# A last block whose gates change from Sigmoid to exponential and logarithm, and out weights in rotating slots, in a chain of linear attention, a gated layer and soft mixture of experts

## The chip, the cores and the metric

The kernel runs on 1 core of one Trainium2 chip. The metric is the device time of one execution in microseconds. A core has five engines with a queue each: TensorE (PE; PEld is its weight loading), VectorE (DVE), ScalarE (ACT), GpSimd (POOL) and SyncE (SP). Each queue runs its instructions in the order in which they were written; semaphores hold an instruction until what it reads or overwrites is ready. DMA transfers are started from SP's and ACT's queues.

## The reference

Three stages follow each other, all in fp32, on 4 sequences of 576 tokens:

```python
# attention: 4 x 8 heads, 64 wide, 128 features
h = einsum(x * scale, omega) - sum((x * scale)**2) / 2
phi = exp(h - max(h)) / sqrt(128)                 # for q and for k
kv, z = k_phi^T v, sum(k_phi)
x = (q_phi kv) / (q_phi z + 1e-6)                 # 2304 tokens x 512
# gated layer, 512 -> 1536 -> 512
gate = 1 / (1 + exp(-(x @ w_gate)))
x = (gate * (x @ w_val)) @ w_out
# soft mixture of experts: 8 experts, 4 slots each
logits = x @ phi
d, c = softmax of logits over tokens, softmax of logits over slots
slot_in = d.T @ x
slot_out[e] = relu(slot_in[e] @ w1[e]) @ w2[e]
out = c @ slot_out
```

`w_gate`, `w_val` and `w_out` arrive as 8-byte floats and are narrowed in the kernel.

## The kernel before

The 2304 tokens are cut into blocks: four of 512 (blocks 0 to 3, each the first 512 tokens of a sequence) and block 4 of 256, the last 64 tokens of each sequence. The attention works on 16 units of two heads (u = 0 to 15). The gated layer has 12 slices of 128 of its hidden dimension (f = 0 to 11). Nearly all its products are exact to fp32 by splitting each operand into a high part (rounded to fp32r) and a low part (the rest), and taking three products (`three`). A weight piece (`wscr[f]`, part 0 gate, 1 value, 2 out) is loaded into `WR`, six slots of 512 columns shown as `ws`, then split by a cast (`hi_of`, on ACT or DVE) and a subtraction (`lo_of`, on POOL or DVE).

The order is: attention for units 0 to 3, then block 0 for f < 6, block 1, block 0's other f (GROUPS; interleaved with the later units), then blocks 2 and 3 together as a pair (`pair_jobs`), then block 4, the last block (steps i >= LAST), then the experts. In `pair_jobs`, six steps of two f each make gate and value for both blocks with seven products in place of eight (`pair_up`), and block 2's out products. Then a stretch planned at SPAND = 33 us makes block 3's out products alone, for which the out weights of all f are loaded once more in pairs (`pair_load(f, 2, at)` into slots at and at + 1). At its end come the first loads of the last block's pieces (`load_part(k)` into slot k). In the last block each piece that has been split starts the load of the piece six later in its place.

A gate of the blocks before 2 is made from the sum `s` in PSUM by absolute value, exponential, logarithm, one DVE operation and an exponential: exp(min(s, 0) - ln(1 + exp(-abs(s)))). The pair and the last block use ACT's Sigmoid. ACT holds one table of functions at a time; an `ACT_TABLE_LOAD` changes it. Its first table, natural_log_exp_and_others, is loaded by name at the start; all other loads are put in by the compiler where the next function isn't in the table. Exponentials of the experts' softmax (`chunk_logits`, `weights`, `join_slots`, `last_slots`) stand among the Sigmoids.

The order on each queue is not that of the code. Every operation is recorded with its reads, its writes and a due time (`plan.t` less a lead), and a list scheduler (`Plan.schedule`) runs them in a model with a cost for each and gives each engine the ready operation that is due first; ACT's change of table is in it (RELOAD). The whole order is then issued from one line, which is why L425 is the line of every instruction in the profile. Names tell them apart: `ga` and `va` are the banks of gate and value, `o0` to `o3` those of the out products, `fl` others; `ga_a` the gate in SBUF (and, in the pair, split out weights of odd f), `gt` the gated product in two parts, `w0` to `w2` the split weights; `x2T` and `x` (x2) a block's result and its transposed copy, brought back by 16 DMAs of SP (`chunk_back`). The experts' first weights w1 are loaded from ACT's queue, w2 from SP's.

The gate in the last block and the choice of slots before:

```python
        if i >= LAST:
            ACT.activation(out=a, in_=ps, func=AF.Sigmoid)
            return a
...
        places = [4, 2, 0, 4, 2, 4]
```

At the tail (`last_slots`), block 4's logits, their maximum, the exponential of `dt` (ACT), the slots' sums `ps` in bank o0 and then the experts follow each other; a few products without use (`warm`, bank va) are put between.

Of the kernel before, what the change touches and what calls it, by code (L numbers as in the profile page):

```python
# [20 lines left out]
B, H, S, D, M = 4, 8, 576, 64, 128  # L21
# [3 lines left out]
NF = DFF // 128  # L25
# [7 lines left out]
PAIR = (2, 3)  # L33
# [12 lines left out]
W_LO = float(np.uint32(0x38000000).view(np.float32))  # L46
BIG = 3.0e38
W_HI = float(np.uint32(0x47EFFFFF).view(np.float32))

# [31 lines left out]
READY = 12.0  # L81
EARLY = 6.0
LEAD = {
# [28 lines left out]
class Plan:  # L112
# [135 lines left out]
    def schedule(self):  # L248
# [109 lines left out]
        while ev:  # L358
# [13 lines left out]
            for e in E:  # L372
                while free_at[e] <= now + 1e-9:
# [21 lines left out]
                    c, held = self.cost(e, alt[1], alt[3], outs, ins)  # L395
                    want = {AF.Exp: 0, AF.Ln: 0, AF.Sigmoid: 1}.get(alt[3].get("func"), table) if e == "ACT" else table
                    if want != table:
                        c, table = c + RELOAD, want
# [33 lines left out]
def body(ctx, tc, nc, qkT, tok, von, omT, wall, phi, w1, w2, ident_d, srep_d, rrep_d, mask_d, out):  # L432
# [87 lines left out]
    Vs = [carve(g3, 896 * k + 128, [NT, 2, 64]) for k in range(2)]  # L520
    QTF = carve(g3, 2560, [2, S])
    obf = carve(g3, 3712, [256])
    QY = carve(g3, 1792, [512])
    HKs = [carve(r, 0, [4, 2, M]) for r in (g4, q2)]
# [110 lines left out]
    def chunk_qT(u, i):  # L635
        if u >= N_SPLIT and i < 2:
            turn_q(u, i)
            return
        ps = bank().rearrange("p (h n) -> p h n", h=2)
        n, k = ((256, 0), (256, 0), (64, 64))[i]  # L640
        for h in range(2):
            if i == 2:
                PE.transpose(ps[:, h, 0:128], HTs[u % 2][:, 0, h, :], ident)
                continue
            for t in range(2):
                PE.transpose(ps[:, h, 128 * t:128 * t + 128], HQs[u % 2][:, 2 * i + t, h, :], ident)
        if u < N_NUM:
            copy(QTF[:, :, 256 * i:256 * i + n], ps[:, :, k:k + n], SITE["hqt"])
            return
        qh, ql = (QT[:, l, :, 256 * i:256 * i + n] for l in range(2))  # L650
        hi_of(qh, ps[:, :, k:k + n], SITE["hqt"])
        lo_of(ql, ps[:, :, k:k + n], qh, ("DVE",))

    def turn_q(u, h):

        y = QY.rearrange("p (j t a) -> p t j a", j=4, t=4)
        for t in range(4):
            DVE.transpose(y[:, t], HQs[u % 2][:, t, h].rearrange("p (j a) -> p j a", j=4))
        scr = qscr[2 * (u % 2) + h]
        SP.dma_start(out=scr, in_=QY)  # L660
        d = scr.rearrange("(i a) (j f) -> j a i f", i=4, j=4)
        for j in range(4):
            SP.dma_start(out=QTF[32 * j:32 * j + 32, h, 0:512].rearrange("p (i f) -> p i f", i=4), in_=d[j])
        x = QTF[:, h, 0:512].rearrange("p (i t b) -> p t i b", t=4, i=4)
        qh, ql = (QT[:, k, h, 0:512].rearrange("p (t i b) -> p t i b", t=4, i=4) for k in range(2))
        hi_of(qh, x, SITE["hqt"])
        for t in range(4):
            lo_of(ql[:, t], x[:, t], qh[:, t], ("DVE",))
# [58 lines left out]
    def step_chunks(u):  # L727
# [3 lines left out]
        def P(i):  # L731
            return lambda: chunk_proj(v, i)

        def kv():
            chunk_kv(u)
            prep_qk(v, 1)
            load_unit(u + 2)
# [7 lines left out]
        if v < ROWS:  # L745
            c = [kv, P("K0"), qT[0], P("K1"), qT[1], qT[2], P("T"), num[0], P("Q0"), num[1], last]
            own = (0, 2, 4, 5, 7, 9)
        else:
            c = [kv, P("K"), qT[0], qT[1], qT[2], P("T"), num[0], num[1], last]
            own = (0, 2, 3, 4, 6, 7)  # L750
# [96 lines left out]
    def gate(i):  # L847
        n = BLOCKS[STEPS[i][0]][1]
        ps = up_passes(i, 0, "ga")
        a = T([128, 512], "ga_a", F32, 2)[:, 0:n]  # L850
        if i >= LAST:
            ACT.activation(out=a, in_=ps, func=AF.Sigmoid)
            return a
# [168 lines left out]
    def chunk_logits(j):  # L1022
# [13 lines left out]
        DVE.tensor_scalar(out=neg, in0=new, scalar1=-1.0, scalar2=None, op0=ALU.mult)  # L1036
        DVE.tensor_copy(out=lt[0:p, 1, :], in_=ps)
        ACT.activation(out=lt[0:p, 0, :], in_=ps, func=AF.Exp, bias=neg, accum_out=row)
        if j != DONE[0]:
# [83 lines left out]

    def load_w1():

        e = len(W1)
        if e < E:
            W1.append(pieces(EXTAGS[e], 3 if EXTAGS[e] == "XT" else 1))
            for c in range(4):
                ACT.dma_start(out=W1[e][c], in_=w1[e, :, 1024 * c:1024 * c + 1024])  # L1130

    def load_w2():
# [209 lines left out]
    stream("att", T0)  # L1342
    ACT.preload_act_table_set("natural_log_exp_and_others")
    DVE.memset(g4[:, 0:256], 0.0)
# [106 lines left out]
    def pair_jobs(t):  # L1451
# [34 lines left out]
        for n in range(6):  # L1486
            f, t0 = 2 * n, t + dt * n
            add(t0, lambda f=f, t0=t0: pair_up(f, 0, t0, 0.39 * dt))
            add(t0 + 0.01, lambda f=f: (f + 2 < NF and pair_load(f + 2, 0, 0), pair_split(1)))
            add(t0 + 2.11, lambda f=f: split_out(f, 4))  # L1490
            add(t0 + 0.39 * dt, lambda f=f, t0=t0: pair_up(f, 1, t0 + 0.39 * dt, 0.39 * dt))
            if n < 5:
                add(t0 + 0.39 * dt + 0.01, lambda f=f: (pair_load(f + 2, 1, 2), pair_split(0)))
            add(t0 + 0.39 * dt + 0.02, lambda f=f: split_out(f + 1, 4))
            downs(f, t0 + 0.9 * dt, PAIR[0], "a")
            downs(f + 1, t0 + 1.01 * dt, PAIR[0], "a")
            add(t0 + 0.4 * dt, lambda f=f: pair_load((f + 2) % NF, 2, 4))
        t += SPANQ
        places = [4, 2, 0, 4, 2, 4]
        dt = SPAND / NF  # L1500
        for n in range(6):
            f, at, t0 = 2 * n, places[n], t + SPAND * n / 6
            if n in (0, 1):
                add(t + 0.2 + 0.1 * n, lambda f=f, at=places[n + 1]: pair_load(f + 2, 2, at))
            add(t0 + 0.02, lambda f=f, at=at: (split_out(f, at), late_split(f)))
# [3 lines left out]
            downs(f + 1, t0 + 0.06 + 2 * dt, PAIR[1], "b")  # L1509
            nxt = {0: lambda: pair_load(6, 2, 4), 1: lambda: pair_load(8, 2, 2), 3: lambda: pair_load(10, 2, 4),  # L1510
                   2: lambda: (load_part(0), load_part(1)), 4: lambda: (load_part(2), load_part(3)),
                   5: lambda: (load_part(4), load_part(5))}[n]
            add(t0 + 0.035, nxt)
        add(t + SPAND - 6.0, lambda: (split_w(LAST, 0), split_w(LAST, 1)))
# [10 lines left out]
    for g, (j, f0, f1) in enumerate(GROUPS):  # L1525
        span = SPAN[g]
        if j == NB - 1:
            m2_jobs(0, start + 3.0, 60.0)
            jobs += [(start + 4.0, "ex", load_w1), (start + 12.0, "ex", load_w1)]
            start = pair_jobs(start)  # L1530
            jobs += [(start - SPAND + 1.0 + 8 * k, "ex", load_w1) for k in range(4)]
            m2_jobs(PAIR[0], start - SPAND + 1.0, SPAND * 0.9)
            m2_jobs(PAIR[1], start + span / NF, span * 0.7)
            jobs += [(start - 5.0, "ex", load_w1), (start + 2.0, "ex", load_w1), (start + 8.0, "ex", free_more),
                     (start + span * 0.9, "end", free_halves), (start + span * 0.85, "m2", join_slots)]
# [99 lines left out]
```

## Time and profile before

| | us |
|---|---|
| median of 3 runs | 669.59 |
| lowest and highest of them | 668.32, 669.80 |
| the profiled execution | 666.81 |
| its span, from the first to the last instruction | 664.9 |
| TensorE busy in it | 644.0 |
| VectorE, ScalarE, GpSimd busy in it | 479.7, 410.6, 289.2 |

The profile is of one execution. Its times count from the start of the span. Matmuls are pipelined, so that neighbouring entries overlap and a busy TensorE need not be at its peak. "Idle before" is the time that an engine waited ahead of an instruction, and the name behind the arrow is what ended the wait.

### The profile page before, as it was taken

What the parts mean: (1) busy time and instruction counts of PE and PEld (TensorE: products, weight loads), DVE (VectorE), ACT (ScalarE), POOL (GpSimd) and SP (SyncE); (2) the same over time, 40 slices, a digit from 0 to 9 for tenths busy, and PEclk for the clock granted to TensorE, in tenths of its full rate; (3) what the DMA queues carried; (4) which work ended last, traced back from release to release, by engine and by line L of the source; (5) the groups of instructions that cost most, each with busy time, mean ns of one, the idle gap of its engine ahead of it and who ended that gap; (6) DMA issues with size and microseconds to landing.
All of it is one profiled execution on the core that took longest, in us unless ns stands there. A gap on an engine that the chain in (4) does not pass through costs nothing.

```text
span 664.9 us, 12634 instructions
## 1 busy us (share of the span) xinstructions
PE 644.0 (97%) x4268; PEld 513.2 (77%) x4268; DVE 479.7 (72%) x1379; ACT 410.6 (62%) x937; POOL 289.2 (43%) x272
## 2 busy tenths in 40 slices
PE   7899999999999999999999999999999999899995
PEld 5676777768888888888877778878888779899663
DVE  5898989888998765667689987557557757756323
ACT  4899989889998866777675654534442225445012
POOL 0456344455445344455453555555551453542100
PEclk9999999999999999999999999999999999999998
DMA  7987857678976345223315552222228899777988
GB/s 233 324 269 260 274 188 273 204 237 272 298 260 215 101 115 176 90 97 98 109 49 185 195 147 78 63 64 63 65 65 293 278 316 346 229 233 264 353 334 240
DMA packets 55216, 132.17 MB, mean 199 GB/s; under 512 B 6256, under 2 KB 14192, under 8 KB 55152
## 3 DMA queue, kind: packets, MB, share of 16 engines
q1 hardware_dynamic: 49328, 114.01, 52.7%
q10 hardware_dynamic: 5824, 17.37, 7.7%
q8 instruction: 33, 0.54, 0.3%
q14 instruction: 31, 0.25, 0.1%
HBM read 113.00 MB, written 14.16 MB: 191 GB/s over the span
## 4 chain that ended last, share of the span: by engine, by line
PE 84%; DMA 5%; DVE 4%; ACT 2%; POOL 1%; SPq 1%; issue 1%; DVEq 0%; POOLq 0%; ACTq 0%
PE o L425 24%; PE fl L425 23%; PE va L425 19%; PE ga L425 18%; DMA g<-in_tok 2%; DMA x2T<-x 1%; DMA g<-in_w 1%; DVE g L425 1%; DMA ws<-wscr 1%; SPq L425 1%; DVE XT L425 1%; POOL g L425 1%; DVE ga_a L425 1%; ACT w L425 0%; DMA g<-in_qkT 0%
## 5 line engine op out<-in xcount | busy, mean ns | idle before, releaser
L425 POOL TENSOR_TENSOR w<-ws,w 128x512 fp32r<-128x512 f32 (+1 forms) x101 | 120.6, 1195 | 161.3 <-ACT w L425 67.2
L425 PE MATMUL o<-gt,w 128*128 128x512 f32 (+1 forms) x576 | 134.7, 372 | 2.2 <-POOL w L425 0.9
L425 PEld LDWEIGHTS o<-gt,w 128*128 128x128 f32 x576 | 97.2, 189 | 24.4 <-issue 2.4
L425 PE MATMUL ga<-XT,w 128*128 128x512 f32 (+1 forms) x432 | 101.6, 367 | 0.9 <-POOL XT L425 0.9
L425 ACT ACTIVATE w<-ws 128x512 fp32r<-128x512 f32 (+1 forms) x100 | 57.7, 579 | 72.3 <-PE o L425 28.1
L425 PE MATMUL va<-XT,w 128*128 128x512 f32 (+1 forms) x432 | 100.1, 366 | 1.6 <-DVE ga_a L425 1.1
L425 PE MATMUL fl<-g,g 64*128 64x128 f32 (+4 forms) x686 | 84.1, 313 | 3.5 <-ACT g L425 1.7
L425 ACT ACTIVATE g<-g 128x128 f32<-128x128 f32 (+4 forms) x206 | 73.8, 414 | 16.9 <-DVE g L425 12.9
L425 PEld LDWEIGHTS ga<-XT,w 128*128 128x128 f32 x432 | 69.9, 189 | 16.8 <-issue 4.7
L425 PEld LDWEIGHTS va<-XT,w 128*128 128x128 f32 x432 | 70.5, 189 | 15.2 <-issue 2.4
L425 PEld LDWEIGHTS fl<-g,g 64*128 64x128 f32 (+2 forms) x686 | 60.3, 182 | 24.4 <-issue 7.3
L425 ACT ACTIVATE x2T<-g 128x512 f32<-128x512 f32 x72 | 45.8, 666 | 4.2 <-DVE x L425 2.4
L425 ACT ACTIVATE g1b<-g1b,g 128x128 f32<-128x128 f32 x128 | 40.8, 389 | 5.9 <-DVE g L425 5.7
L425 DVE TENSOR_SCALAR x2T<-x2T 128x512 f32<-128x512 f32 (+1 forms) x72 | 35.9, 513 | 3.7 <-ACT x2T L425 3.4
L425 POOL TENSOR_TENSOR g<-g 128x640 f32<-128x640 f32 (+1 forms) x19 | 23.4, 1230 | 33.3 <-DMA g<-in_tok 13.3
L425 DVE CUSTOM_DVE_ANT_0 g<-fl,g 128x128 f32<-128x128 f32 x142 | 32.3, 286 | 6.5 <-PE fl L425 6.4
L425 PE MATMUL o<-gt,ga_a 128*128 128x512 f32 x144 | 35.4, 393 | 0.0
L425 DVE TENSOR_TENSOR XT<-fl,XT 128x512 f32<-128x512 f32 x24 | 16.6, 690 | 23.0 <-PE fl L425 23.0
L425 POOL TENSOR_TENSOR x<-x2T 128x512 int32<-128x512 int32 x19 | 24.6, 1295 | 16.1 <-DVE x2T L425 11.3
L425 PEld LDWEIGHTS o<-gt,ga_a 128*128 128x128 f32 x144 | 26.7, 188 | 5.8 <-POOL ga_a L425 0.3
L425 ACT ACTIVATE ga_a<-ga_a 128x512 f32<-128x512 f32 x48 | 30.0, 624 | 1.7 <-DVE ga_a L425 1.4
L425 POOL TENSOR_TENSOR w<-x,w 128x512 fp32r<-128x512 f32 x15 | 19.3, 1285 | 24.2 <-DVE x2T L425 11.5
(254 smaller groups left out, 1264.3 us busy)
## 6 DMA issues: line engine op xcount, KB each, us to landing
ws<-wscr SPq DMA_DIRECT2D x42, 512.0 KB, 3.7
g<-in_wall SPq DMA_DIRECT2D x36, 512.0 KB, 5.0
ws<-wscr SPq DMA_DIRECT2D x54, 256.0 KB, 3.7
wscr<-x SPq DMA_DIRECT2D x36, 256.0 KB, 4.6
g<-in_qkT SPq DMA_DIRECT2D x15, 576.0 KB, 5.3
g<-in_tok SPq DMA_DIRECT2D x15, 576.0 KB, 5.1
g<-in_w ACTq DMA_DIRECT2D x16, 512.0 KB, 6.9
XT<-in_w ACTq DMA_DIRECT2D x12, 512.0 KB, 4.6
```

The source lines that it names most:

```text
L425: ins = getattr(self.eng[e], method)(*a, **k)
```

## The change

The Sigmoids of the last block become the chain of the earlier blocks: `i >= LAST` becomes `LAST <= i < SIGS` with SIGS = 0. The table for exponential and logarithm is loaded by name once, ahead of block 2's logits' exponential, recorded as reading their sum and `SG[1]`, which the pair's last Sigmoid writes. Block 3's out weights and the first pieces of the last block go round the three pairs of slots in turn. In the attention, the third chunk of q transposes (the tail's) comes first from unit 3 on; code for a turn through DRAM is cut in two, for units from 16 on. Some numbers get names, with the values that they had.

```diff
+EXP_LN = "natural_log_exp_and_others"
...
-EARLY = 6.0
+SIGS = 0
+W1AT = (1.0, 9.0, 17.0, 25.0, 28.0, 35.0)
+W1FLOOR = (0, 0, 0, 0, 0, 0)
+EARLY = 6
+M2A = -32.0
+M2B = 0.66
+M2C = 3.75
+M2D = 0.7
...
                     want = {AF.Exp: 0, AF.Ln: 0, AF.Sigmoid: 1}.get(alt[3].get("func"), table) if e == "ACT" else table
+                    want = 0 if alt[1].startswith("preload") else want
...
-    QTF = carve(g3, 2560, [2, S])
-    obf = carve(g3, 3712, [256])
-    QY = carve(g3, 1792, [512])
+    QTF = carve(g3, 2688, [2, S])
+    obf = carve(g3, 3840, [256])
+    QYs = carve(g3, 1792, [2, 512])
+    QLs = carve(g3, 2816, [2, 512])
...
         if u >= N_SPLIT and i < 2:
-            turn_q(u, i)
+            split_q(i)
             return
...
         def kv():
+            if u >= N_SPLIT:
+                turn_q(u, 0)
+                turn_q(u, 1)
             chunk_kv(u)
...
-            c = [kv, P("K"), qT[0], qT[1], qT[2], P("T"), num[0], num[1], last]
+            c = [kv, P("K"), qT[2], qT[0], qT[1], P("T"), num[0], num[1], last]
...
-        if i >= LAST:
+        if LAST <= i < SIGS:
             ACT.activation(out=a, in_=ps, func=AF.Sigmoid)
             return a
         ACT.activation(out=a, in_=ps, func=AF.Abs)
...
         DVE.tensor_copy(out=lt[0:p, 1, :], in_=ps)
+        if j == PAIR[0] and SIGS < NS:
+            plan.place([("ACT", "preload_act_table_set", (EXP_LN,), {})], [lt[0:p, 0, :]], [ps, SG[1]])
         ACT.activation(out=lt[0:p, 0, :], in_=ps, func=AF.Exp, bias=neg, accum_out=row)
...
-            add(t0 + 0.01, lambda f=f: (f + 2 < NF and pair_load(f + 2, 0, 0), pair_split(1)))
+            add(t0 + 0.01, lambda f=f: (pair_load(f + 2, 0, 0) if f + 2 < NF else pair_load(2, 2, 0), pair_split(1)))
...
-            if n < 5:
-                add(t0 + 0.39 * dt + 0.01, lambda f=f: (pair_load(f + 2, 1, 2), pair_split(0)))
+            add(t0 + 0.39 * dt + 0.01, lambda f=f: (pair_load(f + 2, 1, 2), pair_split(0)) if f + 2 < NF else pair_load(4, 2, 2))
...
-        places = [4, 2, 0, 4, 2, 4]
+        places = [4, 0, 2, 4, 0, 2]
...
-            if n in (0, 1):
-                add(t + 0.2 + 0.1 * n, lambda f=f, at=places[n + 1]: pair_load(f + 2, 2, at))
...
-            nxt = {0: lambda: pair_load(6, 2, 4), 1: lambda: pair_load(8, 2, 2), 3: lambda: pair_load(10, 2, 4),
-                   2: lambda: (load_part(0), load_part(1)), 4: lambda: (load_part(2), load_part(3)),
-                   5: lambda: (load_part(4), load_part(5))}[n]
-            add(t0 + 0.035, nxt)
+            if n < 3:
+                add(t0 + 0.035, lambda f=f, at=at: pair_load(f + 6, 2, at))
+            else:
+                add(t0 + 0.035, lambda at=at: (load_part(at), load_part(at + 1)))
```

## Rows read from the trace of the kernel before

**Rows 1.** The page's head, TensorE: busy us (share of the span), instructions.

```profile
PE 644.0 (97%) x4268; PEld 513.2 (77%) x4268; DVE 479.7 (72%) x1379; ACT 410.6 (62%) x937; POOL 289.2 (43%) x272
```

**Rows 2.** Stretches: length, busy PE, PEld, DVE, ACT, POOL, clock, DMA share, GB/s.

```profile
60.00:70.00 10.00, 8.41 (x56) 6.93 (x57) 9.29 (x38) 9.41 (x25) 7.11 (x8) 1.00 0.85 284
560.00:580.00 20.00, 17.70 (x141) 16.92 (x141) 14.62 (x35) 10.69 (x18) 9.49 (x8) 1.00 0.80 224
585.70:607.30 21.60, 21.60 (x181) 20.63 (x180) 13.58 (x30) 10.02 (x17) 9.94 (x8) 1.00 0.66 216
```

**Rows 3.** Who TensorE waited for in 500 to 620: us, times, longest.

```profile
PE va L425 <- DVE ga_a L425: 1.1, 1, 1.1
PE o L425 <- POOL w L425: 0.9, 2, 0.7
PE va L425 <- POOL w L425: 0.5, 1, 0.5
```

**Rows 4.** TensorE's instructions in time: start us, us, operation, count, idle before.

```profile
538.41 2.56 PE L425 MATMUL o<-gt,w 128*128 128x512 f32 x10 [0.46 <-DVE w L425]
...
585.68 1.60 PE L425 MATMUL ga<-XT,w 128*128 128x256 f32 x12
...
591.45 1.60 PE L425 MATMUL va<-XT,w 128*128 128x256 f32 x12
...
614.13 1.06 PE L425 MATMUL va<-dt 128*128 128x128 f32 x8
615.34 1.97 PE L425 MATMUL o<-dt,x 128*128 128x32 f32 x16
```

**Rows 5.** ScalarE's groups after 512, up to 340, whole, in 560 to 572.

```profile
L425 ACT ACT_TABLE_LOAD x9 | 11.5, 1283 | 1.5 <-PE o L425 1.3
...
L425 ACT ACT_TABLE_LOAD x1 | 1.3, 1283 | 0.7 <-PEq L1630 0.7
L425 ACT ACTIVATE ga_a<-ga_a 128x512 f32<-128x512 f32 x44 | 27.5, 624 | 1.6 <-DVE ga_a L425 1.2
L425 ACT ACTIVATE ga_a<-ga_a,one_b 128x512 f32<-128x512 f32 x22 | 15.7, 716 | 0.2
...
L425 ACT ACTIVATE ga_a<-ga 128x256 f32<-128x256 f32 x12 | 4.6, 382 | 5.5 <-PE ga L425 4.7 <-DVE w L425 0.8
...
L425 ACT ACT_TABLE_LOAD x4 | 5.1, 1283 | 0.2
```

**Rows 6.** ScalarE's instructions in time.

```profile
330.15 0.62 ACT L425 ACTIVATE w<-ws 128x512 fp32r<-128x512 f32 x1
...
535.80 1.15 ACT L425 ACTIVATE w<-ws 128x512 fp32r<-128x512 f32 x2 [1.56 <-DMA ws<-wscr]
...
577.40 0.63 ACT L425 ACTIVATE w<-ws 128x512 fp32r<-128x512 f32 x1 [5.91 <-DMA ws<-wscr]
...
607.90 0.38 ACT L425 ACTIVATE ga_a<-ga 128x256 f32<-128x256 f32 x1
...
613.74 1.28 ACT L425 ACT_TABLE_LOAD   x1
615.03 0.26 ACT L425 ACTIVATE dt<-dt 128x64 f32<-128x64 f32 x1
```

**Rows 7.** VectorE: a group's count, busy time and mean; then instructions in time.

```profile
L425 DVE CAST gt<-ga_a 128x256 fp32r<-128x256 f32 x11 | 6.0, 547 | 0.2
...
575.98 0.43 DVE L425 CAST w<-ws 128x512 fp32r<-128x512 f32 x1 [2.26 <-DMA ws<-wscr]
...
588.84 0.42 DVE L425 TENSOR_TENSOR ga_a<-va,ga_a 128x256 f32<-128x256 f32 x1 [0.87 <-PE va L425]
589.29 0.29 DVE L425 CAST gt<-ga_a 128x256 fp32r<-128x256 f32 x1
...
614.24 0.22 DVE L425 TENSOR_TENSOR dt<-o,cs 128x64 f32<-128x64 f32 x1
```

**Rows 8.** Who SyncE's queue waited for in 559 to 564: us, times, longest.

```profile
SPq L425 <- DMA g<-in_w: 3.2, 2, 2.5
```

More of the change, by code (lines that the diff above doesn't have):

```diff
@@ L654, in turn_q @@
     def turn_q(u, h):
-        y = QY.rearrange("p (j t a) -> p t j a", j=4, t=4)
+        y = QYs[:, h].rearrange("p (j t a) -> p t j a", j=4, t=4)
         for t in range(4):
@@ L659, in turn_q, with split_q @@
         scr = qscr[2 * (u % 2) + h]
-        SP.dma_start(out=scr, in_=QY)
+        SP.dma_start(out=scr, in_=QYs[:, h])
         d = scr.rearrange("(i a) (j f) -> j a i f", i=4, j=4)
         for j in range(4):
-            SP.dma_start(out=QTF[32 * j:32 * j + 32, h, 0:512].rearrange("p (i f) -> p i f", i=4), in_=d[j])
-        x = QTF[:, h, 0:512].rearrange("p (i t b) -> p t i b", t=4, i=4)
+            SP.dma_start(out=QLs[32 * j:32 * j + 32, h].rearrange("p (i f) -> p i f", i=4), in_=d[j])
+    def split_q(h):
+        x = QLs[:, h].rearrange("p (i t b) -> p t i b", t=4, i=4)
         qh, ql = (QT[:, k, h, 0:512].rearrange("p (t i b) -> p t i b", t=4, i=4) for k in range(2))
@@ L1122, in pieces, with load_w1 @@
         return [t[:, 1024 * c:1024 * c + 1024] for c in range(n)]
-    def load_w1():
+    def load_w1(k=None):
         e = len(W1)
+        plan.floor = 0.0 if k is None else W1FLOOR[k]
         if e < E:
@@ L1130, in load_w1 @@
                 ACT.dma_start(out=W1[e][c], in_=w1[e, :, 1024 * c:1024 * c + 1024])
+        plan.floor = 0.0
     def load_w2():
@@ L1342, in body @@
     stream("att", T0)
-    ACT.preload_act_table_set("natural_log_exp_and_others")
+    ACT.preload_act_table_set(EXP_LN)
     DVE.memset(g4[:, 0:256], 0.0)
@@ L1530, in body @@
             start = pair_jobs(start)
[L1531 to L1534, printed above, removed]
+            jobs += [(start - SPAND + x, "ex", lambda k=k: load_w1(k)) for k, x in enumerate(W1AT)]
+            m2_jobs(PAIR[0], start + M2A, span * M2B)
+            m2_jobs(PAIR[1], start + M2C, span * M2D)
+            jobs += [(start + 8.0, "ex", free_more),
                      (start + span * 0.9, "end", free_halves), (start + span * 0.85, "m2", join_slots)]
```

## The prediction

> **What bounds the kernel now.** I read the page's head first: TensorE is busy 97% of the span [rows 1]. So only time in which TensorE waits can come back; the change takes no matmul away. Then the table by stages says where it waits: 1.6 of 10 us at the start around 60 to 70, 2.3 of 20 in 560 to 580, and nothing in 585.7 to 607.3 [rows 2]. The waits of TensorE in 500 to 620 name the releasers: 1.1 us for VectorE's product `ga_a`, 0.9 and 0.5 for GpSimd's low parts of weights [rows 3]. These 2.5 us are the waits of 560 to 585; TensorE's own list adds one of 0.46 for VectorE's low part at 538.41 [rows 4]. Together 3.0 us: about all that the out-weight slots and the gates can win on TensorE ahead of the tail.
>
> The profiled execution took 666.81 us, 1.91 more than its span; the median of the runs shown is 669.59, 2.78 above it. I make the sum as a difference on the profiled execution and set it on the median.
>
> **Table loads.** After 512 us the trace has 9 loads of ScalarE's function tables at 1283 ns; in the first 340 us it has 1, though 22 gates ran there with exponential, logarithm and exponential again [rows 5]: the table loaded there by name holds both. So one load by name should serve the whole end, and 8 of the 9 go: 8 x 1.28 = 10.3 us of ScalarE. ScalarE has slack there, so the sum looks at where a load holds something up.
>
> At the tail, the load of 613.74 ends where the exponential of `dt` starts, 615.03 [rows 6]. Its input was ready at 614.24 + 0.22 = 614.46 [rows 7]. TensorE starts the slot products at 615.34, behind 8 warming matmuls that end at 614.13 + 1.06 = 615.19 [rows 4]. Without the load the products could start near 614.8. If the order keeps the warming ahead, 615.34 - 615.19 = 0.15 is won; if not, 615.34 - 614.8 = 0.5. I take -0.3, between them. A switch cost 615.03 - 613.74 = 1.29 us there [rows 6]. The Trainium skill (ScalarE: Activation LUTs, What ACT_TABLE_LOAD costs) counts some 2.66 us for each switch to another set, a drain included. The trace shows no such drain behind this load; by that figure the tail's term would be larger by 1.4 us at most, and the sum -2.9.
>
> At the last gate, two loads with one small exponential between, 2.6 us, put its Sigmoid at 607.90 [rows 6]. The chain below is 1.9 us longer than a Sigmoid and so takes less than the loads' place: 0, with no gain either, since the out products and the joining of the slots cover it.
>
> The load by name stands in ScalarE's queue ahead of the exponential of block 2's logits, behind the last Sigmoid. It takes the place of the first of the 9, and block 3's out products cover it on TensorE: 0. Behind it in the queue wait casts of out weights; were that cover gone, it would cost 1.28.
>
> **The gates of the last block.** Each of 12 Sigmoids (382 ns [rows 5]) becomes an absolute value, an exponential, a logarithm, a VectorE operation and an exponential. Durations by rows: the absolute value as the Sigmoid, which reads the same bank, 0.38. For the exponential at half the width of 624 ns [rows 5], between 0.31 (half) and 0.62, I take 0.41, nearer half, as the Sigmoid of 256 columns lies. The logarithm adds 716 - 624 = 0.09 [rows 5]: 0.50. VectorE's part as its product of the same shape, 0.42 [rows 7]. ScalarE gains 12 x (0.41 + 0.50 + 0.41) = 15.8 us and loses 10.3; VectorE gains 12 x 0.42 = 5.0. The stretch 585.7 to 607.3 holds five steps of 4.32 us, with ScalarE busy 10.0 / 5 = 2.0 a step and VectorE 2.7 [rows 2]; 1.32 and 0.42 more still fit. So throughput doesn't bind; latency may.
>
> The latency, with 0.2 for each change of engine (an allowance): 0.2 + 0.38 + 0.41 + 0.50, less two overlaps of 0.1, + 0.2 + 0.42 + 0.2 + 0.41 = 2.5 us from the gate's last matmul; then 0.2 + 0.42 for the product with the value: 3.1. In the step at 585.68 the gate's matmuls end at 587.28; the value's bank must be free for the next value's matmuls at 591.45, 4.17 later [rows 4]. Today the product begins at 588.84, 1.56 after [rows 7], and hides all of the Sigmoid. Slack is left, 1.0 us. But ScalarE takes other work between the links: in a present gate a cast of 330.15 stands between the first two, and holds the second for 0.52 (0.62 less the overlap of 0.1) [rows 6]. Two of these use the slack up. And VectorE's casts of the gated product average 547 ns where a quick one takes 0.29 [rows 7]: 0.26 of waiting inside the instruction. So the bounds are 0 (all fits) and 12 x 0.26 = 3.1 us (two casts between, and the waiting passes through each time). I take +0.5, nearer the lower, since both engines are about half idle there.
>
> **Block 3's out weights.** The six pair transfers keep number and size, and those of f = 0, 2 and 4 leave at the same moments as now, as slots come free in the last pair's step; only the slots differ. Later, the pair for f = 10 goes where f = 4 and 5 come free, and the last block's first two pieces where 6 and 7 do; now it is the other way round. What this does for 538.41: ScalarE's casts at 535.80 (the first for the second of those pieces) had waited 1.56 us for a transfer [rows 6]; the cast of f = 8 stood behind it in the same queue, and the out product waited 0.46 for its low part [rows 4]. With those pieces later, f = 8 goes first: -0.46. Bounds: -0.46, and +0.5 if the same wait returns in front of f = 10. The moved transfers have the out products of four more f ahead of the first gate of the last block to cover them: 0; without that cover, the 1.56 that the cast waits now.
>
> **The waits of 560 to 585.** They come from late weights: ScalarE's cast at 577.40 had waited 5.91 us for a transfer [rows 6], VectorE's at 575.98 2.26, with the product that frees the value's bank queued behind it [rows 7]. The transfers were late because SyncE's queue stood 3.2 us for earlier w1 transfers in 559 to 564 [rows 8], with block 3's transposed transfers between. On ScalarE, 4 loads, 5.1 us, fall into 560 to 572 [rows 5], where the casts that free ring slots queue behind them; two or three gates there add 2.6 to 4.0. If ScalarE was the cause, all 2.5 goes; if it was SyncE's queue, none. Both are seen, so I take half: -1.25. Another pile-up would add as much as the longest now, +1.1, so the bounds are -2.5 and +1.1.
>
> **Attention.** N_SPLIT is 16 and there are 16 units, so `turn_q` and `split_q` never run, and the moved carvings touch nothing else. What remains is that the tail's transposes come first from unit 3 on. TensorE waits 1.6 us around 60 to 70 [rows 2], where unit 3 ends and block 0's tokens are due. A copy of 512 columns (as one of the gate's, 0.6) becomes the late one instead of a short one: bounds -1.6 and +0.6; I take 0. The budgets rewritten with names (`W1AT`, `M2A` and so on) give the same numbers: 0.
>
> **Sum.** -0.3 - 0.46 + 0.5 - 1.25 = -1.5 us: 665.3 for the profiled execution, 668.1 for the median.
>
> **Rivals.** A: about this sum, 667.3 to 668.8. B, the late weights stay: SyncE's wait for w1 transfers speaks for it, the full ScalarE in 560 to 572 against; -0.3 - 0.46 + 0.5 = -0.3, 669.3, no change. C, all waits go and the gates fit: -0.5 - 0.46 - 2.5 = -3.5, 666.1. D, slower: the chain of a gate passes 4.17 us after its matmuls' end, with two casts between links and VectorE held; from there each excess goes straight to TensorE. The slack of 1.0 against two casts of 0.52 speaks for it; that both engines are half idle, against. +3.1 - 0.3 - 0.46 = +2.3, 671.9. E, the table doesn't hold: a load ahead of each logarithm and one behind, 2.6 us a gate, takes ScalarE to 2.0 + 1.32 + 2.6 = 5.9 a step against 4.32, 12 x 1.6 = +19, 689. The 22 gates without loads speak against it.
>
> **How the numbers follow.** A 0.36, B 0.30, C 0.17, D 0.15, E 0.02. Apart from no change is what exceeds 0.2%, 1.34 us (under 668.25 or over 670.93), about what a measurement of this kernel can tell. A is faster in some three quarters of its range (0.27), C in all (0.17), B in a small part, where attention's order adds a gain (0.04): 0.48. D and E are slower, 0.17, and B by mishap 0.01: 0.18. The rest, 0.34, is no change. The range reaches to C below and to the lower part of D above: 665.6 to 671.3, which leaves out E, the upper D and the lowest C, under 2 in 10.
>
> **What would show it.** One table load after 512 us, near 518, none in 560 to 616; 36 activations and 12 VectorE operations more; no wait near 538; the waits of 560 to 585 halved; the slot products about 0.3 earlier after the last out product. Wrong would be TensorE waiting for `ga_a` or the value's bank in each step of the last block (D), or for low parts of weights as long as now, with SyncE's queue held by w1 transfers (B).

## The result, and the profile after

The changed kernel takes 678.04 us (median of 4 runs, 676.98 to 681.18) against 669.57 for the kernel before on the same chip (4 runs): ratio 1.0138, 95% interval 1.0101 to 1.0175. It is slower by 8.5 us between the medians, or 1.4%; the prediction was 668.1, faster by 1.5. The profiled execution took 681.18 us with a span of 678.8, 13.9 more than the 664.9 of before. It is the slowest of the four, as that of before lies at the fast end of its runs, so that the traces show some 5 us more than the medians.

The head of the page, and then the table by stretches (length, busy PE, PEld, DVE, ACT, POOL, granted clock, DMA share, GB/s), to be held against [rows 1, 2]:

```profile
PE 648.5 (96%) x4268; PEld 516.9 (76%) x4268; DVE 479.2 (71%) x1398; ACT 417.7 (62%) x967; POOL 280.1 (41%) x263
```

```profile
60.00:70.00 10.00, 8.63 (x60) 6.59 (x58) 8.95 (x28) 9.31 (x22) 4.73 (x5) 1.00 0.96 332
357.00:367.00 10.00, 7.80 (x28) 6.01 (x27) 6.07 (x8) 4.04 (x7) 8.26 (x5) 0.83 0.74 239
540.00:560.00 20.00, 13.35 (x54) 9.59 (x52) 7.41 (x12) 2.61 (x5) 4.25 (x3) 0.83 0.75 228
560.00:580.00 20.00, 19.90 (x172) 18.21 (x168) 14.30 (x36) 11.82 (x29) 11.51 (x9) 1.00 0.94 290
585.70:607.30 21.60, 19.20 (x147) 18.99 (x147) 11.86 (x28) 13.90 (x31) 8.68 (x7) 0.92 0.78 239
```

TensorE has as many matmuls as before. Two new holes stand out: 2.2 of 10 us in 357 to 367, and 6.6 of 20 in 540 to 560. In both the granted clock is 0.83 on average, so part of the stretch ran at the lower of the two levels. In the same stretches of before TensorE was busy 9.04 and 19.92 at clock 1.00. A third hole, 2.4 of 21.6, lies in 585.7 to 607.3 at clock 0.92, where before had none [rows 2].

To add this up I cut every trace at the same matmuls of TensorE: the first and last of the pair's gate and value products, the first of block 2's logits, the first gate of the last block, the first of block 4's logits, and the slot products. A stage is the time between two of them. This is the main table of the study; it also holds the runs told below. The stages of each line come from one profiled execution, which can lie off its kernel's median: that of e1 took 680.5 us with a median of 674.6, that of e10 666.5 with 669.7.

| us | pair | block 3 | last block | to slot products | ratio of run times [95%] |
|---|---|---|---|---|---|
| before | 145.4 | 31.1 | 63.7 | 3.9 | 1 |
| after | 150.0 | 39.2 | 65.4 | 3.6 | 1.0138 [1.0101, 1.0175] |
| e1_no_slots | 149.3 | 38.1 | 64.1 | 3.6 | 1.0099 [1.0071, 1.0128] |
| e2_no_q | 145.4 | 38.5 | 65.1 | 3.6 | 1.0105 [1.0073, 1.0136] |
| e3_no_gates | 150.0 | 36.3 | 63.0 | 3.9 | 1.0099 [1.0064, 1.0135] |
| e4_slots_alone | 145.3 | 36.4 | 65.3 | 3.9 | 1.0089 [1.0060, 1.0118] |
| e5_attention_alone | 148.6 | 32.4 | 63.4 | 3.9 | 1.0035 [1.0014, 1.0056] |
| e6_gates_alone | 145.4 | 37.0 | 62.8 | 3.6 | 1.0032 [0.9999, 1.0064] |
| e7_cast_later | 145.4 | 35.4 | 71.1 | 3.6 | 1.0116 [1.0050, 1.0182] |
| e8_no_w1_traffic | 145.4 | 31.2 | 76.8 | 3.6 | one run, 694.6 us |
| e9_gates_w2_later | 145.4 | 34.2 | 69.7 | 3.6 | 1.0119 [1.0094, 1.0143] |
| e10_gates_w1_w2_later | 145.3 | 30.2 | 65.8 | 3.6 | 1.0023 [1.0004, 1.0042] |
| e11_before_w2_later | 145.4 | 37.1 | 65.3 | 3.9 | 1.0096 [1.0068, 1.0124] |
| e12_before_both_later | 145.3 | 31.2 | 65.8 | 3.9 | 1.0016 [1.0000, 1.0032] |
| e13_no_attention_both_later | 145.3 | 37.0 | 69.3 | 3.6 | 1.0100 [1.0080, 1.0119] |
| e14_all_both_later | 148.9 | 37.5 | 69.8 | 3.6 | 1.0143 [1.0117, 1.0170] |
| e15_attention_low_parts_dve | 147.8 | 33.4 | 64.8 | 3.9 | 1.0026 [1.0003, 1.0049] |
| e16_casts_and_both_later | 145.4 | 30.8 | 69.0 | 3.6 | 1.0030 [1.0002, 1.0058] |

From before to after: 4.6 in the pair, 8.1 in block 3's stage, 1.7 in the last block, less 0.3 to the slot products: 14.1, the difference of the spans (13.9) up to rounding; ahead of the pair, and from the slot products to the end (49.5 in both), nothing changed.

**Block 3's stage.** TensorE's, VectorE's, ScalarE's, SyncE's and GpSimd's instructions there, in time (start, duration, operation, count, idle before):

```profile
542.01 0.39 PE L434 MATMUL o<-gt,w 128*128 128x512 f32 x1
548.38 0.79 PE L434 MATMUL o<-gt,w 128*128 128x512 f32 x1 [5.98 <-DVE gt L434]
549.84 4.12 PE L434 MATMUL o<-gt,w 128*128 128x512 f32 x10 [0.67 <-POOL w L434]
```

```profile
547.29 0.43 DVE L434 CAST w<-ws 128x512 fp32r<-128x512 f32 x1 [7.38 <-DMA ws<-wscr]
547.64 0.69 DVE L434 TENSOR_TENSOR gt<-g1a,gt 128x512 fp32r<-128x512 f32 x1
```

```profile
537.68 0.34 ACTq L434 DMA_DIRECT2D XT<-in_w  x1
...
540.81 0.34 ACTq L434 DMA_DIRECT2D XT<-in_w  x1
548.12 0.63 ACT L434 ACTIVATE w<-ws 128x512 fp32r<-128x512 f32 x1 [7.96 <-DMA ws<-wscr]
```

```profile
535.82 4.07 SPq L434 DMA_DIRECT2D x2T<-x  x6
540.68 0.81 SPq L434 DMA_DIRECT2D ws<-wscr  x2
542.26 0.33 SPq L434 DMA_DIRECT2D more<-in_w  x1
```

```profile
548.46 1.33 POOL L434 TENSOR_TENSOR w<-ws,w 128x512 fp32r<-128x512 f32 x1 [9.46 <-DVE gt L434]
```

VectorE's cast at 547.29 is that of the last block's first piece. SyncE asked for this piece at 540.68, behind six transposed transfers; it landed 6.6 us later, with w1 transfers of 512 KB from ScalarE's queue under way since 537.68. Behind the cast in VectorE's order stands the low part of block 3's gated product (547.64), which has nothing to do with that piece, and for which TensorE waits 5.98 us. The wait of 0.67 behind it has the same source: GpSimd makes the low part of that f's weights only at 548.46, although ScalarE's cast for it had ended by 540.2, because in this program it waits there for VectorE's low part (547.64). Then ten matmuls take 4.12 us; the same ten took 2.56 at full clock [rows 4]. The mean clock was 0.57 from 549.84 to 553.80. Two matmuls of the same product took 0.39 and 0.79, and together 0.61 in before:

```profile
537.34 0.61 PE L425 MATMUL o<-gt,w 128*128 128x512 f32 x2
```

So the stage loses 5.98 + 0.67 in waits and 1.56 + 0.57 in slower matmuls, less the wait of 0.46 that before had there [rows 4]: 8.3 us, where the table has 8.1.

**The pair.** GpSimd's and TensorE's instructions there:

```profile
355.80 5.70 POOL L434 TENSOR_TENSOR g<-XT,g 128x1024 fp32r<-128x1024 f32 x2 [2.73 <-ACT g L434]
```

```profile
361.55 0.50 PE L434 MATMUL fl<-g,w 128*128 128x512 f32 x1 [2.20 <-POOL g L434]
...
362.55 2.34 PE L434 MATMUL va<-g,w 128*128 128x512 f32 x5
```

GpSimd makes two low parts of the pair's tokens in 5.70 us, the second of which TensorE waits for. In the kernel before, VectorE made these two, and TensorE's waits around this place, 0.8 and 0.2, were for other things. In 345 to 430 TensorE now waits 2.2, 0.6 and 0.5, 3.3 in all, against 1.0 before; a clock of 0.83 over 10 us is, as an estimate, at most 1.7 more. That is up to 4.0 of the 4.6.

**The gates.** ScalarE's groups from 480 to the end (busy, mean ns, idle before), VectorE's from 560 to 626, and the start of the slot products:

```profile
L434 ACT ACTIVATE ga_a<-ga_a 128x256 f32<-128x256 f32 x24 | 9.8, 410 | 1.6 <-DVE ga_a L434 1.5
L434 ACT ACTIVATE ga_a<-ga_a,one_b 128x256 f32<-128x256 f32 x12 | 6.1, 508 | 0.4
L434 ACT ACTIVATE ga_a<-ga 128x256 f32<-128x256 f32 x12 | 4.6, 383 | 8.1 <-PE ga L434 7.5 <-PE o L434 0.6
...
L434 ACT ACT_TABLE_LOAD x1 | 1.3, 1283 | 0.0
```

```profile
L434 DVE CAST gt<-ga_a 128x256 fp32r<-128x256 f32 x12 | 7.0, 580 | 0.3
...
L434 DVE SCALAR_TENSOR_TENSOR ga_a<-ga,ga_a 128x256 f32<-128x256 f32 x12 | 5.0, 416 | 7.3 <-ACT ga_a L434 7.3
```

```profile
628.42 1.06 PE L434 MATMUL va<-dt 128*128 128x128 f32 x8
629.32 1.87 PE L434 MATMUL o<-dt,x 128*128 128x32 f32 x16
```

One load of a table is left where nine were [rows 5]; the three functions take 383, 410 and 508 ns. The slot products start 3.6 us after block 4's logits instead of 3.9.

### The profile page after: what moved, and what is told of

It reads as the page before. It is cut to its first block, busy times and chain, and to the rows that moved or that the text cites. A ratio compares the mean times of both kernels' runs of the same rounds, so it can differ in the third digit from the quotient of the medians.

```text
span 678.8 us, 12670 instructions
## 1 busy us (share of the span) xinstructions
PE 648.5 (96%) x4268; PEld 516.9 (76%) x4268; DVE 479.2 (71%) x1398; ACT 417.7 (62%) x967; POOL 280.1 (41%) x263
## 4 chain that ended last, share of the span: by engine, by line
PE 77%; DVE 8%; DMA 6%; POOL 3%; ACT 2%; issue 2%; SPq 1%; DVEq 0%; POOLq 0%; ACTq 0%
PE o L434 22%; PE fl L434 20%; PE va L434 18%; PE ga L434 17%; DMA ws<-wscr 3%; DMA g<-in_tok 3%; DVE XT L434 2%; DVE g L434 2%; POOL g L434 2%; SPq L434 1%; DVE x2T L434 1%; ACT ga_a L434 1%; DVE gt L434 1%; ACT g L434 1%; DVE ga_a L434 1%
## 5 line engine op out<-in xcount | busy, mean ns | idle before, releaser
L434 PE MATMUL o<-gt,w 128*128 128x512 f32 (+1 forms) x576 | 138.0, 378 | 7.6 <-DVE gt L434 6.3
L434 PEld LDWEIGHTS o<-gt,w 128*128 128x128 f32 x576 | 98.8, 192 | 30.0 <-DVE gt L434 7.1
L434 ACT ACTIVATE w<-ws 128x512 fp32r<-128x512 f32 (+1 forms) x102 | 59.1, 580 | 71.3 <-PE o L434 29.6
L434 ACT ACTIVATE ga_a<-ga_a 128x512 f32<-128x512 f32 (+1 forms) x72 | 39.8, 553 | 6.5 <-DVE ga_a L434 6.2
L434 DVE TENSOR_SCALAR x2T<-x2T 128x512 f32<-128x512 f32 x72 | 38.5, 540 | 1.1 <-ACT x2T L434 1.0
L434 POOL TENSOR_TENSOR g<-g 128x512 f32<-128x512 f32 (+1 forms) x19 | 21.9, 1154 | 26.8 <-DMA g<-in_tok 19.2
L434 POOL TENSOR_TENSOR w<-x,w 128x512 fp32r<-128x512 f32 x17 | 21.8, 1285 | 24.7 <-ACT w L434 8.8
L434 ACT ACTIVATE ga_a<-ga 128x512 f32<-128x512 f32 (+1 forms) x36 | 18.8, 522 | 19.2 <-PE ga L434 18.5
```

Of the source, the lines that this page charges most:

```text
L434: ins = getattr(self.eng[e], method)(*a, **k)
```

## The experiments

No run leaves out part of the computation.

**One part taken out of the change (e1 to e3).** The diffs, on the changed kernel: e1 takes the hunks of `pair_jobs` back, e2 and e3 are

```diff
-            c = [kv, P("K"), qT[2], qT[0], qT[1], P("T"), num[0], num[1], last]
+            c = [kv, P("K"), qT[0], qT[1], qT[2], P("T"), num[0], num[1], last]
```

```diff
-SIGS = 0
+SIGS = NS
```

e1: 

> The changed kernel with the old out-weight slots; gates and attention order stay changed. Theory S (slots: behind the new rotation the last block's first two pieces are asked for after all 16 transposed transfers, and their cast holds VectorE ahead of the out product's low part): the 6.0 and 0.7 us waits near 542 to 550 and the slow clock behind them go, about 8 of the 9 us; 669 to 671. Rival A (the attention's order lost 4.6 us ahead of 513): the time falls only by some 4, to about 674. Rival G (the gates' chain): the time stays at 676 or above.

e2: 

> The changed kernel with the attention's old order of transposes. Theory S: the queues around block 3 keep the same order as in the changed kernel, so its 6 us wait stays; 676 to 678. Rival A: the 4.6 us lost ahead of block 2's last out products come back; about 673.5.

e3: 

> The changed kernel with the Sigmoids in the last block and no table loaded by name. Theory S as I hold it: the cast of the last block's first piece now stands in ScalarE's queue and not in VectorE's, behind the cast for f = 8 but ahead of that for f = 9, so a wait of some 3 to 6 us stays near f = 9; 673 to 677. Rival G: the gates cost 2 us in the last block, and the slots nothing by themselves; about 670.

Each gives back only 0.3 to 0.4%, by intervals that overlap the whole change's. e1 took 674.6 as rival A has it, but its stage is 38.1 without the slots, so theory S fails; e2's 675.3 lies between its theories; e3's 675.6 is in its range. The pair's stage is long in exactly the runs that have attention's order, and block 3's stage is long with the gates (e1), with the slots (e3) and with both (e2). So no single part is the cause, and slots and gates do not add: either of them makes the stage 5 to 7 us longer, both together 7 to 8.

**One part alone on the kernel before (e4 to e6).** The same hunks, put into the kernel before.

e4: 

> The kernel before with the new slots alone. Theory S: slower by 3 to 6 us, 672 to 676, with a wait near block 3's f = 8 or 9 and the transfers of the last block's first pieces behind 16 transposed ones. Rivals A and G: 669 to 670, no change.

e5: 

> The kernel before with the attention's new order of transposes alone. Theory A2: it costs 4.4 us in the pair of blocks 2 and 3, where GpSimd gets two low parts of 1024 columns of the pair's tokens ahead of TensorE's need and the clock drops behind the wait; that stage 149 to 150 us instead of 145.5, in all 672 to 674. Rival: the loss needs the other parts too; 668 to 670.

e6: 

> The kernel before with the new gates and the table by name alone. Theory Q (late transfers of weights in block 3's stage): the new plan asks for f = 10's out weights behind two 512 KB pieces of w2, so the stage from block 2's logits to the first gate of the last block takes 36 to 38 us instead of 31, and the whole 672 to 675; the last block itself stays within 1.5 us of before. Rival G (the chain of a gate is too long): the last block takes 66 us or more instead of 63.7, and block 3's stage 31 to 32.

All three are slower, or at best the same (the gates' interval touches 1). e4 came out in its range with 674.7. e5's pair is 148.6 as forecast for A2, but its whole, 670.9, is below A2's 672, and the drop of the clock that A2 expected did not come: it is 1.00 in 357 to 367. e6's stage is that of theory Q, with the whole just under it, at 671.9. In the traces the gates alone lose 5.9 us in block 3's stage, and win 0.9 in the last block, which may be chance, and 0.3 to the slot products, which every run with the gates has. What they did to block 3's stage, by SyncE's, ScalarE's and TensorE's queues:

```profile
536.57 1.08 SPq L434 DMA_DIRECT2D more<-in_w  x2
537.76 17.04 SPq L434 DMA_DIRECT2D ws<-wscr  x8
```

```profile
545.71 0.63 ACT L434 ACTIVATE w<-ws 128x512 fp32r<-128x512 f32 x1 [7.09 <-DMA ws<-wscr]
```

```profile
546.40 0.73 PE L434 MATMUL o<-gt,w 128*128 128x512 f32 x2 [2.32 <-ACT w L434]
547.75 4.63 PE L434 MATMUL o<-gt,w 128*128 128x512 f32 x10 [0.62 <-POOL w L434]
```

The last pair of out weights is asked for at 537.76, as early as in the kernel before, but behind both 512 KB pieces of w2 (`more`) instead of between them, with a w1 transfer following at 538.02. It lands 7.9 us later, and TensorE waits and then runs ten matmuls in 4.63 us. The planner put the table load in front of the logits' exponential and so moved two casts of out weights from VectorE to ScalarE and the transfers behind them. The planner that stands in the kernel, run by itself without the chip, shows that it is the load: with the load by name and the Sigmoids kept, all five queues have e6's order up to the end of this stage, and with the new gates and no load by name they have that of before. Its own end time foresaw little of what was measured: 628.97 before, 629.30 with the gates, 628.97 with the slots, 630.96 with attention's order, 631.37 with all three.

**Order of the casts, or transfers (e7, e8).** Both on e2:

```diff
-        add(t + SPAND - 6.0, lambda: (split_w(LAST, 0), split_w(LAST, 1)))
+        def first_split():
+            plan.floor = 519.0
+            split_w(LAST, 0)
+            split_w(LAST, 1)
+            plan.floor = 0.0
+        add(t + SPAND - 6.0, first_split)
```

```diff
-W1AT = (1.0, 9.0, 17.0, 25.0, 28.0, 35.0)
-W1FLOOR = (0, 0, 0, 0, 0, 0)
+W1AT = (58.0, 58.1, 58.2, 58.3, 58.4, 58.5)
+W1FLOOR = tuple(464.0 + x for x in W1AT)
```

e7: 

> The changed kernel with the attention's old order, and the casts of the last block's first two pieces placed some 4.5 us later in the plan, behind the out product's parts of f = 8 and 9; the transfers are asked for as before. Theory Q: VectorE no longer stands with the product's low part behind it, the 4.3 us wait of e2 goes; block 3's stage 32 to 34 instead of 38.5 and the whole 669 to 671. Rival T (the transfers are too slow whatever waits for them): the wait moves to f = 10 or the first gate, the stage stays at 36 or more; 673 to 676.

e8: 

> A look at one stage: as e2, but all w1 transfers that ran in block 3's stage are held back until the last block. The end gets much slower for it (the whole 690 to 705), only block 3's stage is compared. Theory T (the w1 traffic makes the weights' landing 6 us and more): the last block's first pieces land within 4 us and the stage takes 31 to 33. Theory Q alone (the order of the queues): casts of these pieces still stand ahead of out products, the stage takes 35 or more.

Without w1 transfers the stage is 31.2, as before; with late casts alone 35.4, so that e7 fits neither of its theories, and its last block, 71.1, holds one wait of 5.8 for `x2T`. This seemed to settle on the transfers. But in e8 every transfer of the stage leaves earlier too: the last block's first piece at 532.63 in place of 536.23 (e2), and `more` some 7 us earlier. The piece took 5.75 us to land even without w1 beside it, not the 4 at most that theory T had. So e8's short stage goes with transfers that were asked for earlier, and it does not show that those of w1 slow the others.

**The large transfers held (e9 to e11).** e9 and e11 hold `more` in the plan, on e6 and on the kernel before; e10 holds w1 as well:

```diff
-        plan.floor = plan.t
+        plan.floor = 523.0
...
-W1FLOOR = (0, 0, 0, 0, 0, 0)
+W1FLOOR = (0, 0, 0, 521.0, 521.5, 0)
```

e9: 

> The gates and their table load alone on the kernel before, with the two 512 KB transfers of `more` held in the plan until the reloads of block 3's out weights and the first pieces of the last block are asked for. Theory: with the gates alone the 6 us in block 3's stage come from these two transfers, which went ahead of the last pair of out weights, so that pair's landing took about 8 us. Then block 3's stage is 31 to 33 us (37.0 with the gates alone, 31.1 before), and the whole 667 to 669.5, at or just under the kernel before, since the gates win some 0.9 us in the last block and 0.3 at the tail. Rival: the w1 transfers from ScalarE's queue, which now leave a little earlier, keep the landings long by themselves; the stage stays 36 to 38 and the whole near 672.

e10: 

> As the run with the `more` transfers held, and the w1 transfers that leave in block 3's stage (XT and g0) held some 9 us as well. Theory that either kind of large transfer lengthens the landings: the stage is 31 to 32 us, the shortest of the variants with gates, and the whole 666.5 to 669 unless the held w1 transfers delay pieces of the last block (63 us in it with the gates alone); in that case the last block takes 66 to 72 and the whole is slower than 670. Rival, that the new table load and the casts' new order alone hold TensorE: the stage stays 36 to 38.

e11: 

> The kernel before with the two `more` transfers held in the same way and nothing else changed: a control. If the transfers matter only where they go ahead of the last pair, block 3's stage stays 31 us and the whole within 0.2% of before (0.46 us of waiting at most is there to win). If holding them is a gain by itself, whatever the gates are, it is faster by more than 0.3%.

e11 was a control and missed: with nothing of the change in it, moving two transfers by some 10 us costs 0.96%, as much as the slots and more than the gates. The w1 transfers then moved up into the place of `more`: two leave ahead of 533, where the kernel before had none, and the casts of the last block's pieces wait 7.14 us:

```profile
531.88 0.33 ACTq L425 DMA_DIRECT2D XT<-in_w  x1
...
532.69 0.34 ACTq L425 DMA_DIRECT2D XT<-in_w  x1
540.09 1.15 ACT L425 ACTIVATE w<-ws 128x512 fp32r<-128x512 f32 x2 [7.14 <-DMA ws<-wscr]
```

With both kinds held the stage with gates is 30.2, the shortest of all, and TensorE has no wait of 0.2 or more in 500 to 560. The whole is still 1.0023, with a wait of 2.2 for a gate's `ga_a` in the last block, a stage that is 3.0 longer than in e6. By their intervals the wholes of e10 and e6 can't be told apart, so no gain from the mended stage shows in the time. e9, with w2 alone held, misses both its theories: the stage is 34.2, and the last block loses 5.7 us to one wait for `x2T`.

**Both held, in the other variants (e12 to e14), and both causes mended (e16).** The same two edits on the kernel before (e12), on e2 (e13), on the whole change (e14); e16 is e13 with e7's edit.

e12: 

> The kernel before (Sigmoids, old slots, old order of the attention) with both `more` and the w1 transfers of block 3's stage held as in the run with the gates: a control. If the timing of the large transfers is the whole cause, the stage is 30 to 31.5 us as with the gates, and the whole within 0.3% of before. If the gates' order of the queues is what the holding mends, the control shows a stage as long as with w2 alone held, 36 to 38.

e13: 

> The change without attention's order, with both kinds of large transfer held. If their timing is the whole cause, block 3's stage falls from 38.5 to 30 to 32 us, and the whole from 675.3 to 667 to 670. Rival: the new slots alone make the casts of the last block's first pieces stand in front of out products; then the stage stays at 34 or more, and the whole at 672 or more.

e14: 

> The whole change with both kinds of large transfer held. If the two causes add up, the pair stage stays 149 to 150 us (4.4 more than before), block 3's stage is 30 to 33, and the whole is 671 to 673. Rival, that attention's order also spoils block 3's stage (0.7 us more with it than without it): the stage stays 35 or more, the whole 675 or more.

e16: 

> The change without attention's order, with both kinds of large transfer held, and with the casts of the last block's first two pieces put 4 us later in the plan, behind the parts of f = 8 and 9. Theory that both causes are needed together: with the casts late and the transfers as they were the stage was 35.4 us, with the transfers held and the casts as they were 36.9; with both it is 30.5 to 32, and the whole 668 to 671. Rival, that the new slots ask for the weights too late in any order: 34 us or more, and the whole 673 or more.

(The 36.9 in the last text is 37.0 in the table.) e12 shows that the holding is nearly harmless by itself (1.0016), with a last block of 65.8. e13 went against the theory that the transfers are the whole cause. VectorE's and TensorE's instructions in it, and then VectorE's in e16:

```profile
535.74 0.43 DVE L434 CAST gt<-g1a 128x512 fp32r<-128x512 f32 x1 [1.64 <-PE o L434]
539.85 0.43 DVE L434 CAST w<-ws 128x512 fp32r<-128x512 f32 x1 [3.69 <-DMA ws<-wscr]
540.19 0.69 DVE L434 TENSOR_TENSOR gt<-g1a,gt 128x512 fp32r<-128x512 f32 x1
```

```profile
540.93 0.49 PE L434 MATMUL o<-gt,w 128*128 128x512 f32 x1 [2.29 <-DVE gt L434]
542.66 4.64 PE L434 MATMUL o<-gt,w 128*128 128x512 f32 x10 [1.23 <-POOL w L434]
```

```profile
535.51 0.43 DVE L434 CAST gt<-g1a 128x512 fp32r<-128x512 f32 x1 [1.64 <-PE o L434]
535.97 0.69 DVE L434 TENSOR_TENSOR gt<-g1a,gt 128x512 fp32r<-128x512 f32 x1
```

In e13 the piece is not slow: SyncE gets to it after 537.02 and it has landed by 539.85. But the cast stands between the two parts of one gated product, and 3.69 us of waiting are enough. In e16 the low part follows its cast, and the stage is 30.8. e7 mended the first casts' place alone (35.4), e13 the transfers alone (37.0), e16 both: the two had to be mended together. The last block is then 69.0 (3.1 of it one wait for `x2T`), and the whole 1.0030, 671.6 against the 671 at most that was expected: part of the loss moved on. e14's numbers, 37.5 and 678.4, are those that its rival forecast, but e13 has 37.0 without attention's order, so the rival's cause isn't needed: attention's order adds at most 0.5 in block 3's stage.

**Attention's low parts (e15).** On e5:

```diff
-        hi_lo(OT[7], t3)
+        hi_lo(OT[7], t3, ("DVE",))
...
-        hi_lo(OT[3], b22)
+        hi_lo(OT[3], b22, ("DVE",))
```

e15: 

> Attention's new order alone, with the low parts of the pair's tokens for the products 3 and 7 made on VectorE alone, as they were in the kernel before, and not on GpSimd. If they are the cause, the wait of TensorE of 2.2 us at the start of the pair goes, its clock stays full there, and the pair stage is 145.3 to 146.3 us (148.7 with the new order alone, 145.5 before), the whole 668 to 669.5. Rival, that VectorE is as late with them, or another wait takes the place: 148 or more, the whole 670.5 or more.

TensorE's waits in 345 to 430, in e5 and in e15:

```profile
PE fl L425 <- POOL g L425: 2.2, 1, 2.2
PE o L425 <- POOL gt L425: 0.6, 1, 0.6
PE o L425 <- POOL ga_a L425: 0.5, 1, 0.5
```

```profile
PE fl L425 <- DVE g L425: 1.4, 1, 1.4
PE ga L425 <- DVE ga_a L425: 0.2, 1, 0.2
```

It lies between the two theories: the wait falls from 2.2 to 1.4 and the later two go, but the pair's stage is 147.8, not 145.4. VectorE is late as well, since the last unit's products with their divisors come at 350.65, 3.2 us later than before (347.48), while the pair starts 1.1 earlier. What remains is 2.4 us: waits of 1.6 against 1.0, and a clock of 0.83 in 357 to 367, as in the whole change and unlike e5, at most 1.7 by the same estimate. The whole (1.0026) can't be told from e5's.

## Why the prediction was wrong

**Table loads: right.** One load after 512 is left, at 521.98, the pair's delay later than "near 518"; the tail's term of -0.3 is 3.9 - 3.6 = 0.3, in every run with the gates. The Trainium skill (ScalarE: Activation LUTs, What ACT_TABLE_LOAD costs) counts a drain of some 1.4 us with each load; by it the tail would have won, as an estimate, up to 1.4 more, and the trace does not agree: in the kernel before, the activation ahead of the load ends at 613.72, the load runs from 613.74 to 615.02, the next activation starts at 615.03 [rows 6], and the tail won 0.3.

What the tail wins, the last gate takes back. It was put at 0, and in each of the eleven traces with the new gates, the change's included, TensorE waits 0.28 to 0.76 us for the last gated product; in the seven with Sigmoids it does in none:

```profile
624.10 1.69 PE L434 MATMUL o<-gt,w 128*128 128x256 f32 x12 [0.29 <-DVE gt L434]
```

In the change the joining products stand at 618.23, ahead of the last step, and no longer cover it.

**The load by name at nothing: the failed step.** The load itself is covered, as said. But the prediction costed it where it stands and not what it moves: this one instruction shifted two casts and two 512 KB transfers in the planned order, and block 3's stage grew by 5.9 us with the gates alone (e6). With the transfers held it is 30.2 (e10), so that the loss is in the order of the queues and the transfers and not in the gates.

**The gates of the last block: right.** The three functions and VectorE's operation measured 383, 410, 508 and 416 ns, for 0.38, 0.41, 0.50 and 0.42 said. The chain fits: between 595.45 and 608.41 TensorE's steps are 4.32 us, without a wait. VectorE's cast is at 580 ns in place of 547 [rows 7]: 0.4 us over 12. Rival D did not happen, nor E. The net of all gate edits, with the transfers held in both, is 1.0023 against 1.0016 (e10, e12): no difference.

**Block 3's out weights: the other failed step.** -0.46 with bounds to +0.5 became +5.3 (e4). The step that failed is "the moved transfers have the out products of four more f ahead of the first gate of the last block to cover them: 0". The cover holds for the last block's gate, but not for what stands behind the cast in VectorE's in-order queue. The prediction gave the price without cover as 1.56, the cast's old wait; in the whole change it was 7.38 for the cast, 5.98 for TensorE, and 1.56 more by the clock. The wait near 538 did go with the slots alone: in e4 that f's products run from 538.09 without one, but the next f's wait 3.94 us at 544.91, behind a cast that stands 6.81 for a transfer. In the whole change it did not go: the f of that very wait stands 5.98 and 0.67.

**The waits of 560 to 585: half right by chance.** 0.7 is left there, but 2.4 stand at 589.51: 3.1 in all, against 2.5. ScalarE's and TensorE's instructions:

```profile
587.52 0.63 ACT L434 ACTIVATE w<-ws 128x512 fp32r<-128x512 f32 x1 [3.99 <-DMA ws<-wscr]
588.06 0.40 ACT L434 ACTIVATE ga_a<-ga_a 128x256 f32<-128x256 f32 x1
```

```profile
589.51 1.95 PE L434 MATMUL ga<-XT,w 128*128 128x256 f32 x12 [2.40 <-DVE ga_a L434]
```

A gate's second function stands behind a cast that waits 3.99 us for a transfer; a Sigmoid, one function long, could not be cut in two in this way. The prediction allowed for casts between the links, but for short ones. Late weights were B's mechanism, and SyncE's queue its cause; B's time was that of no change, since it let them stay as late as they were.

**Attention at nothing: failed in place and size.** The bounds -1.6 to +0.6 were for 60 to 70, where TensorE's busy time went from 8.41 [rows 2] to 8.63. The cost came 290 us later, where the last unit meets the pair's tokens: +4.6 in the change, +3.2 alone. The wait for the low part is the same 2.2 us in both, and the difference goes with the clock, 0.83 in 357 to 367 in the change and 1.00 in e5, where the same five matmuls take 1.31 us in place of 2.34:

```profile
360.50 0.50 PE L425 MATMUL fl<-g,w 128*128 128x512 f32 x1 [2.19 <-POOL g L425]
...
361.31 1.31 PE L425 MATMUL va<-g,w 128*128 128x512 f32 x5
```

Alone the whole is +0.35%, some 2 us, part of it won back ahead of the pair, which starts 1.0 us earlier in e5.

The three failed steps have one fault in common: each edit was priced by the instructions that it adds, removes or moves, in an order taken as given. Here every edit goes through a planner, and the order of all queues answers to it.

**What stays open.** Why the order that the planner chose for the kernel before is a good one; e11 suggests that it is one spot among worse ones, but no run searched. Executions of one kernel differ by up to 9 us (e6: 665.3 to 674.2), so that a stage's loss in one trace isn't the median's: e6 loses 5.9 in block 3's stage and some 2 by the medians. Why the clock fell behind some waits and not behind others stays open too. No variant was faster than the kernel before.

## What to carry to other kernels

Where a planner or a compiler orders the queues, an edit's price is the difference of the two orders: look for instructions that wait for a transfer and stand ahead of work on the path, in each in-order queue, before adding up durations. A load that is covered for its own consumer is not covered for what is queued behind it. And take a control that moves the transfers without the change: here it cost as much as the change's parts.

## What was not expected of the hardware

The transfers of weights on the page of the changed kernel (count, KB each, median us to landing):

```profile
ws<-wscr SPq DMA_DIRECT2D x42, 512.0 KB, 3.7
...
ws<-wscr SPq DMA_DIRECT2D x54, 256.0 KB, 3.5
```

Pieces and pairs land in some 3.6 us at the median, whatever their size, but the one that decided took 6.6 us in the change (540.68 to 547.29) and the pair that decided 7.9 in e6 (537.76 to 545.71), beside 512 KB transfers of another queue. In e13, with neither kind of 512 KB transfer under way, that same piece landed in 2.8 (537.02 to 539.83). The Trainium skill (Trainium Kernel Development and Optimization, Key Constraints) says that transfers from SyncE's and ScalarE's queues run on the same DMA engines and interleave; e6 and e10 fit this: a cast of e6 stood 7.09 us for a weight, and with the w1 transfers of ScalarE's queue and `more` held (e10) none stood for one longer than 2.8 us in 525 to 600.

A wait of TensorE can cost more than itself, and no run shows when it does. Ten out products took 4.12, 4.63 and 4.64 us behind waits of 5.98 (the change), 2.32 (e6) and 2.29 (e13), and 2.56 at full clock [rows 4]; the mean granted clock of 540 to 550 was 0.66 in e13 and 1.00 in e16, that is between the lower level of 1.2 GHz and the upper of 2.4. But behind e5's wait of 2.19 at 360.50 and e10's of 2.22 at 584.48 the clock stayed at 1.00, while behind a wait of 1.35 in e15 it was 0.83 on average in 357 to 367.

The kernel before itself ran from 663 to 673 us over all chips and runs, 1.5%, with the same program: medians of a few runs hold to some 0.3%, single profiles do not.
